# Converting every weight piece on its own: three X tiles for two, five M tiles for four

## The chip, the core and the metric

The kernel runs on one NeuronCore of a Trainium2 chip. The metric is the device time of one execution in microseconds (us), the median of the runs. The engines named below: PE (TensorE, matrix products and transposes), DVE (VectorE), ACT (ScalarE), POOL (GpSimd) and SP (SyncE, which issues nearly all DMAs here). Each works through its own queue in order; semaphores tie them together.

## What is computed

Attention with normed queries and keys, then a Fourier mixing over sequence and features, then a two-layer feed-forward part, for 8 batches of 448 tokens with 12 heads of 64 (so 768 features and 3072 hidden ones). Cut to what matters:

```python
q_n, k_n = rmsnorm(q, g_q), rmsnorm(k, g_k)
attn = softmax(q_n @ k_n.T / 8)              # per head, 448 x 448
x = attn @ v                                 # heads side by side: 8 x 448 x 768
u = x + real(fft(fft(x, axis=1), axis=2))
un = (u - mean(u)) / sqrt(var(u) + 1e-6)
out = u + relu(un @ w_ch1) @ w_ch2           # 768 x 3072 and 3072 x 768
```

The two weight matrices arrive as float64. Everything else is float32.

## The kernel before

**Work per batch.** `aux(b)` makes batch b's attention, its folding and Fourier step (`spectral`) and the normed rows `un`. `ffn(b)` is the feed-forward part: 24 products `h` (`up`, 18 matmuls each, by a w1 piece) and 36 products `o` (`down`, 12 matmuls each, by a w2 piece). `ffn_input(b, ...)` stands between them: it transposes `un` on PE into the six tiles `unT`, each rounded by ACT and completed by DVE with the remainder, since each float32 factor is split in a high and a low half and every product takes three passes. The program is: `aux(0)` with the first steps of `aux(1)` mixed in, then for each b the parts `ffn(b)` and `aux(b + 1)` merged.

**Weights.** A w1 piece is 128 hidden columns, `(m,)`; a w2 piece is 128 output columns of 512 hidden rows, `(g, d)`. In batch 0 every piece is converted from its double words and stored to HBM (`piece_kept`); later batches load what was stored. The conversion is `bits_of` and then `convert`:

- SP loads the double words into a `wide` tile (tag X; `dbl` in the profile, `dble` for pieces that are converted early, during `aux(0)`), L780;
- ACT makes the absolute high word (L783, into a tile of tag M, `mag` or `mage`) and scales the low word in place (L784);
- DVE clamps (L785), shifts (L789) and merges the sign (L793), and POOL adds the low word (L797); then the X tile is free for the next load;
- ACT rounds the value into the piece's tile (L802), DVE subtracts for the low half (L803), SP stores both halves (L839).

Before, w1 pieces are converted singly (768 values, 1536 words of 4 bytes), but w2 pieces in twos: `w2_doubles(g, d)` loads two neighbouring pieces at once (1024 values, 2048 words), and `value_of` hands the second half to the neighbour from the dictionary `mates`. There are 2 X tiles of 2048 words and 4 M tiles of 1024. From batch 2 on, tags X and M hold the tiles of `fold` as well.

**Order.** The code is written in program order, but a planner that follows a simulated timeline sets the order of each engine's queue, within the dependencies and the tiles that are free. So other tile counts and sizes can move any instruction.

Names: `mag_0_4` is the M tile of piece `(4,)` read for batch 0, `mag_0_0_4` that of piece `(0, 4)`; `mage4_3` is that of the early piece `(4, 3)`. `u0_1`, `un0_1`, `xr0_1` and `x0_100` belong to the four groups of rows of batch 0, `unT0_5` is the sixth transposed tile, `h0_0` and `o0_5_1` are products.

Of the kernel before, what the change touches and what calls it, by code (L numbers as in the profile page):

```python
# [13 lines left out]
U32 = mybir.dt.uint32  # L14
# [77 lines left out]
def spectral_block(ctx, tc, q, k, v, g_q, g_k, w1, w2, d1, d2, out, nb=B):  # L92
# [4 lines left out]
    sb = ctx.enter_context(tc.tile_pool(name="sb", bufs=2))  # L97
# [32 lines left out]
    def behind(ins):  # L130

        others = given.get(ins.ins.engine, [])
        if starting[0] and len(others) > LAG:
            order(
                ins, others[-1 - LAG],
                mybir.DependencyClass.NoSync, mybir.DependencyReason.DATA,
            )
# [15 lines left out]
            turn[0] += 1  # L153
        return ps.tile([128, 512], F32, tag=tag, name=name, bufs=BANKS[tag])

    SLOTS = {"P": 8, "PT": 6, "M": 4, "unT": 6, "h": 6}

    def slot(tag, name, dtype=F32):
        n = 1024 if tag == "M" else 900
        t = sb.tile([128, n], dtype, tag=tag, name=name, bufs=SLOTS[tag])  # L160
        return t if dtype == U32 else t[:, :900]

    def wide(name, dtype=F32):
        return sb.tile([128, 2048], dtype, tag="X", name=name, bufs=2)

    def sub(o, a, b_):
        V.tensor_tensor(out=o, in0=a, in1=b_, op=ALU.subtract)
# [38 lines left out]
    def load_dft():  # L206
        nc.sync.dma_start(D1.rearrange("r i a n -> r (i a n)"), d1)
        st = slot("PT", "d2s")[:N1, : 4 * N1].rearrange("s (n t) -> s n t", n=4)
        for r in rows_of(N1):
            nc.sync.dma_start(st[r], d2[r].rearrange("s (n t) -> s n t", n=4))  # L210
        d2v = D2.rearrange("s i c a t -> s (i c) a t")
        A.copy(d2v[:, :, 0], st)
        sub(d2v[:, :, 1], st, d2v[:, :, 0])
# [166 lines left out]
    def softmax_pair(b, p, Pc):  # L380
        QT, KD, _ = ready[b, p]
        late = b < EARLY
        if late:
            sums[b, p] = sb.tile([C, NC, 2], F32, tag="sums", name=f"sums{b}_{p}")
        for c in range(NC):
            P = slot("P", f"P{b}_{p}_{c}")[:C, : 2 * S]
            Ph = [P[:, :S], P[:, S:]]
            mn = sb.tile([C, 2], F32, tag="mn", name=f"mn{b}_{p}_{c}", bufs=4)
# [51 lines left out]
    def divide_pair(b, p, xT):  # L440

        rs = sums.pop((b, p))
        flat = rs.rearrange("t c h -> t (c h)")
        V.tensor_scalar(out=flat, in0=flat, scalar1=1e-9, scalar2=None, op0=ALU.add)
        V.reciprocal(flat, flat)
        wide_ = slot("PT", f"rs{b}_{p}")[:C, : NC * 128].rearrange(
            "t (c h d) -> t c h d", c=NC, h=2
        )
        G.tensor_copy(wide_, rs[:, :, :, None].broadcast_to([C, NC, 2, D]))
        rt = bank("PT", f"rt{b}_{p}")  # L450
        for c in range(NC):
            nc.tensor.transpose(
                rt[:, c * C : (c + 1) * C],
                wide_[:, c].rearrange("t h d -> t (h d)"), ident[:C, :C],
            )
        V.tensor_tensor(
            out=xT[:, p, :S], in0=rt[:, :S], in1=xT[:, p, :S], op=ALU.mult
        )
# [121 lines left out]
    def fold(b, p, xT, EO):  # L580
# [5 lines left out]
        if kept is not None:  # L586
            eo = slot(kept, f"eo{b}_{p}")
        else:
            if p % 2 == 0:
                halves[b] = wide(f"eo{b}_{p}")  # L590
            eo = halves[b][:, p % 2 * 900 : p % 2 * 900 + 900]
# [174 lines left out]
    w1w, w2w = w1.bitcast(U32), w2.bitcast(U32)  # L766
    kept1 = [dram.tile([128, 2, NR, 128], F32, name=f"w1_{m}") for m in range(NF)]
    kept2 = [dram.tile([128, NR, 2, 4, 128], F32, name=f"w2_{g}") for g in range(NG)]
    def bits_of(src, name):

        _, c, f = src.shape
        bits = slot("M", f"mag{name}", U32)[:, : c * f // 2].rearrange(
            "r (c f) -> r c f", c=c
        )
        raw = wide(f"dbl{name}", U32)[:, : c * f].rearrange(
            "r (c f w) -> r c f w", c=c, w=2
        )
        nc.sync.dma_start(raw.rearrange("r c f w -> r c (f w)"), src)  # L780
        low, high = raw[:, :, :, 0], raw[:, :, :, 1]
        value = bits.bitcast(F32)
        behind(nc.scalar.activation(value, high.bitcast(F32), AF.Abs))  # L783
        behind(nc.scalar.activation(low, low, AF.Copy, scale=2.0**-29))  # L784
        behind(nc.vector.tensor_scalar(  # L785
            out=value, in0=value, scalar1=MIN_HIGH, scalar2=MAX_HIGH,
            op0=ALU.max, op1=ALU.min,
        ))
        behind(nc.vector.tensor_scalar(  # L789
            out=bits, in0=bits, scalar1=5, scalar2=2,  # L790
            op0=ALU.logical_shift_left, op1=ALU.logical_shift_right,
        ))
        behind(nc.vector.scalar_tensor_tensor(  # L793
            out=bits, in0=high, scalar=0xC0000000, in1=bits,
            op0=ALU.bitwise_and, op1=ALU.bitwise_or,
        ))
        behind(nc.gpsimd.tensor_tensor(out=bits, in0=bits, in1=low, op=ALU.add))  # L797
        return value
# [6 lines left out]
        ))  # L805

    early = set()
    mates = {}

    def value_of(p, name):  # L810

        if len(p) == 1:
            return bits_of(w1_doubles(*p), name)
        if p not in mates:
            g, d = p[0], p[1] & ~1
            both = bits_of(w2_doubles(g, d), name)
            for i in range(2):
                mates[g, d + i] = both[:, :, i * 128 : i * 128 + 128]
        return mates.pop(p)

    class Stream:

# [13 lines left out]
        def converted(self, p, name):  # L836
            hl = self.tile(p, name)
            convert(value_of(p, name), [hl[:, k] for k in range(2)])
            nc.sync.dma_start(piece_kept(p), hl.bitcast(F32))  # L839
            return hl  # L840
# [13 lines left out]
    def w1_doubles(m):  # L854
        return w1w[:, m * 256 : (m + 1) * 256].rearrange("(c r) f -> r c f", r=128)

    def w2_doubles(g, d):
        return w2w[g * 512 : (g + 1) * 512, d * 256 : (d + 2) * 256].rearrange(
            "(f r) e -> r f e", r=128
        )  # L860

# [297 lines left out]
```

## Time and profile before

| | |
|---|---|
| median of 3 runs | 2140.9 us (2140.07 to 2142.75) |
| the profiled execution | 2144.78 us, span 2143.0 us |
| PE busy | 2074.9 us (97%) |
| DVE busy | 1548.4 us (72%) |
| ACT busy | 1023.3 us (48%) |
| POOL busy | 342.1 us (16%) |
| mean granted TensorE clock | 0.984 |

Busy time is the union of an engine's instructions. Batch 0's conversions lie between 20 and 440 us of the span; `ffn(0)` begins at 177 us and `ffn(1)` at 431 us. Rows of a waits view say which engine and tile waited for what, with the sum, the count and the longest wait.

### The profile page before, as it was taken

Reading aid. Unit: us, or ns where it says so; the run is one execution under the profiler, and the core shown is the slowest. Engines: PE = TensorE matmul, PEld = TensorE weight load, DVE = VectorE, ACT = ScalarE, POOL = GpSimd, SP = SyncE. Lnnn points to the kernel's source line nnn. Section 1 sums busy time; section 2 is a strip of 40 time slices with the busy share of each in tenths; the row PEclk is TensorE's granted clock in tenths of the full one; section 3 lists DMA queues with packets and bytes.
Section 4 is the critical chain, followed back from the end, with each engine's and each line's share of the span. In section 5 each row is a group of like instructions: output and inputs, shape, how many; then the busy total and the mean of one; then the engine's idle time right before and its main releaser. Section 6 shows DMA issues by size and latency. Waiting matters only on the chain.

```text
span 2143.0 us, 31181 instructions
## 1 busy us (share of the span) xinstructions
PE 2074.9 (97%) x11256; PEld 1846.7 (86%) x11256; DVE 1548.4 (72%) x2948; ACT 1023.3 (48%) x2182; POOL 342.1 (16%) x182
## 2 busy tenths in 40 slices
PE   7877999999999999999999999999999999999998
PEld 4546888889999999999999999999999989999998
DVE  6788888977885878757886778858787578764122
ACT  6857876446542555335542455425553455422100
POOL 3324433311110101001110111101010011000000
PEclk9987999999999999999999999999999999999999
DMA  6538876776566855658555765667556674458874
GB/s 185 184 97 297 275 263 220 269 237 189 174 180 189 235 165 174 187 183 231 156 175 176 240 181 169 179 194 229 166 177 189 190 206 138 152 174 253 233 251 150
DMA packets 283550, 423.86 MB, mean 198 GB/s; under 512 B 181075, under 2 KB 200516, under 8 KB 283396
## 3 DMA queue, kind: packets, MB, share of 16 engines
q1 hardware_dynamic: 278962, 419.75, 63.8%
q10 hardware_dynamic: 4434, 2.11, 0.4%
q8 instruction: 90, 1.47, 0.3%
q14 instruction: 64, 0.52, 0.1%
HBM read 362.01 MB, written 65.31 MB: 199 GB/s over the span
## 4 chain that ended last, share of the span: by engine, by line
PE 81%; DVE 6%; DMA 5%; ACT 3%; issue 2%; POOL 1%; SPq 1%; DVEq 0%; POOLq 0%; ACTq 0%
PE h L1039 29%; PE o L1060 29%; PE S L409 5%; PE av L521 4%; PE pt L509 4%; DMA dbl<-w 2%; PE y L646 2%; PE qk L345 1%; DMA w<-w 1%; PE av L483 1%; DMA ur<-u_dram 1%; ACT P L115 1%; PE oT L996 1%; PE x L677 1%; PE un L908 1%
## 5 line engine op out<-in xcount | busy, mean ns | idle before, releaser
L1039 PE MATMUL h<-unT,w 128*128 128x448 f32 x3456 | 792.0, 372 | 3.4 <-DVE unT L115 1.4
L1060 PE MATMUL o<-hs,w 128*128 128x448 f32 x3456 | 786.4, 371 | 3.1 <-DVE acc L115 1.5
L1039 PEld LDWEIGHTS h<-unT,w 128*128 128x128 f32 x3456 | 638.9, 189 | 57.8 <-DVE unT L115 1.7
L1060 PEld LDWEIGHTS o<-hs,w 128*128 128x128 f32 x3456 | 635.9, 188 | 58.6 <-issue 3.4
L115 ACT ACTIVATE P<-S,mn 112x448 f32<-112x448 f32 x384 | 244.1, 638 | 232.6 <-DVE mn L115 226.7
L115 DVE TENSOR_REDUCE mn<-S 112x1 f32<-112x448 f32 x384 | 232.8, 616 | 47.9 <-PE S L409 38.3
L115 ACT ACTIVATE hs<-h 128x448 fp32r<-128x448 f32 x192 | 104.2, 543 | 299.0 <-PE h L1039 298.2
L115 DVE TENSOR_TENSOR acc<-o,acc 128x448 f32<-128x448 f32 (+1 forms) x240 | 146.9, 614 | 126.6 <-PE o L1060 125.0
L115 DVE SCALAR_TENSOR_TENSOR hs<-h,hs 128x448 fp32r<-128x448 f32 x192 | 119.0, 620 | 139.7 <-ACT hs L115 138.6
L115 POOL TENSOR_TENSOR qkn<-raw 112x1024 f32<-112x1024 f32 x36 | 68.6, 1904 | 679.3 <-PE qk L345 606.1
L115 POOL TENSOR_TENSOR ss<-ss,nhalf 112x16 f32<-112x16 f32 x48 | 142.6, 2972 | 190.2 <-DVE ss L115 167.2
L115 ACT CAST T<-pt 128x448 fp32r<-128x448 f32 x216 | 113.2, 532 | 107.3 <-PE pt L509 105.0
L521 PE MATMUL av<-T,vhl 128*128 128x448 f32 x432 | 151.0, 382 | 0.0
L115 DVE TENSOR_TENSOR T<-pt,T 128x448 fp32r<-128x448 f32 x216 | 131.4, 616 | 25.8 <-ACT T L115 24.7
L115 DVE TENSOR_SCALAR P<-P,sm 112x448 f32<-112x448 f32 x288 | 126.6, 479 | 3.8
L409 PE MATMUL S<-KD,QT 128*112 128x448 f32 x328 | 126.5, 386 | 0.6 <-ACT P L115 0.5
L509 PE MATMUL pt<-ident,P 112*128 112x112 f32 x864 | 124.8, 259 | 0.0
L409 PE MATMUL S<-rounded,QT 128*112 128x448 f32 x328 | 119.9, 366 | 0.0
L509 PEld LDWEIGHTS pt<-ident,P 112*128 112x128 f32 x864 | 103.5, 140 | 16.3 <-DVE R L115 0.3
L115 POOL TENSOR_TENSOR rstd<-st,nhalf 112x1 f32<-112x1 f32 (+2 forms) x32 | 20.2, 632 | 507.7 <-DVE st L115 507.7
L797 POOL TENSOR_TENSOR mag<-mag,dbl 128x768 uint32<-128x768 uint32 (+1 forms) x33 | 75.9, 2301 | 140.6 <-DVE mag L793 93.5
L521 PEld LDWEIGHTS av<-T,vhl 128*128 128x128 f32 x432 | 80.9, 188 | 8.3
(120 smaller groups left out, 2501.4 us busy)
## 6 DMA issues: line engine op xcount, KB each, us to landing
w<-w SPq DMA_DIRECT2D x192, 768.0 KB, 4.9
w<-w SPq DMA_DIRECT2D x288, 512.0 KB, 4.4
dbl<-w SPq DMA_DIRECT2D x20, 768.0 KB, 4.7
dbl<-w SPq DMA_DIRECT2D x13, 1024.0 KB
raw<-q SPq DMA_DIRECT2D x96, 112.0 KB, 3.8
raw<-k SPq DMA_DIRECT2D x96, 112.0 KB, 4.6
values<-v SPq DMA_DIRECT2D x96, 96.0 KB, 4.2
u_dram<-u SPq DMA_DIRECT2D x24, 336.0 KB, 3.8
```

The source lines that it names most:

```text
L115: ins = emit(*args, **kwargs)
L345: nc.tensor.transpose(pt[:, c * C : (c + 1) * C], qk[:, i, c].rearrange("t h d -> t (h d)"), ident[:C, :C],)
L409: ins = nc.tensor.matmul(s_, QT[:, h, cs], K[:, h], start=step == 0, stop=step == 1)
L483: nc.tensor.matmul(av[:, :S], vhl[:, 3 * h + j].rearrange("s h d -> s (h d)"), T, start=h + j == 0, stop=False,)
L509: nc.tensor.transpose(pt[:, c * C : (c + 1) * C], Pc[c][:, 512 * h + j * 128 : 512 * h + (j + 1) * 128], ident[:C, :C],)
L521: nc.tensor.matmul(av[:, :S], lv, T[:, i], start=(j == 0 and i == 0), stop=False)
L646: nc.tensor.matmul(o, src[:, par, t0 : t0 + n], D1[:, ri, par, cols], start=i != 1, stop=i != 0,)
L677: nc.tensor.transpose(xp[:n, i * 128 : (i + 1) * 128], src[:, 3 * half + i], ident)
L797: behind(nc.gpsimd.tensor_tensor(out=bits, in0=bits, in1=low, op=ALU.add))
L908: nc.tensor.transpose(pt[:, OFFS[i] : OFFS[i] + LENS[i]], uns[i][:, p * 128 : (p + 1) * 128], ident[: LENS[i], : LENS[i]],)
L1039: pace(nc.tensor.matmul(o, w[:, a, c], unT[c][:, z], start=n == 0, stop=n == 17))
L1060: pace(nc.tensor.matmul(o, w[:, a, f], hs[4 * g + f][:, z], start=n == 0, stop=n == 11))
```

## The change

Pairs are gone: `w2_doubles` loads one piece (1024 words, 512 KB), `value_of` converts it alone, and `mates` goes. X has three tiles of 1800 words, M has five of 900.

```diff
-    SLOTS = {"P": 8, "PT": 6, "M": 4, "unT": 6, "h": 6}
+    SLOTS = {"P": 8, "PT": 6, "M": 5, "unT": 6, "h": 6}
 
     def slot(tag, name, dtype=F32):
-        n = 1024 if tag == "M" else 900
-        t = sb.tile([128, n], dtype, tag=tag, name=name, bufs=SLOTS[tag])
-        return t if dtype == U32 else t[:, :900]
+        return sb.tile([128, 900], dtype, tag=tag, name=name, bufs=SLOTS[tag])
 
     def wide(name, dtype=F32):
-        return sb.tile([128, 2048], dtype, tag="X", name=name, bufs=2)
+        return sb.tile([128, 1800], dtype, tag="X", name=name, bufs=3)
...
-    mates = {}
 
     def value_of(p, name):
 
         if len(p) == 1:
             return bits_of(w1_doubles(*p), name)
-        if p not in mates:
-            g, d = p[0], p[1] & ~1
-            both = bits_of(w2_doubles(g, d), name)
-            for i in range(2):
-                mates[g, d + i] = both[:, :, i * 128 : i * 128 + 128]
-        return mates.pop(p)
+        return bits_of(w2_doubles(*p), name)
...
     def w2_doubles(g, d):
-        return w2w[g * 512 : (g + 1) * 512, d * 256 : (d + 2) * 256].rearrange(
+        return w2w[g * 512 : (g + 1) * 512, d * 256 : (d + 1) * 256].rearrange(
```

What the planner makes of it, at three places. The line numbers of the changed kernel are smaller by 2 to 8, and the last number of a name only counts tiles.

**ACT's queue at the end of `aux(0)`**, from the first group's last step to the first rounded `unT`. Before:

```order
L115 ACTIVATE xr0_0_1430,st0_2_1466<-un0_2_1480 111x768
L802 CAST w1_0_0_1545<-mag_0_0_1546 128x768
L783 ACTIVATE mag_0_1_1559<-dbl_0_1_1560 128x768
L784 ACTIVATE dbl_0_1_1560<-dbl_0_1_1560 128x768
L115 ACTIVATE un0_1_1511<-u0_1_1495,st0_1_1496 112x768
L783 ACTIVATE mag_0_2_1572<-dbl_0_2_1573 128x768
L784 ACTIVATE dbl_0_2_1573<-dbl_0_2_1573 128x768
L115 ACTIVATE xr0_1_1497,st0_1_1496<-un0_1_1511 112x768
L115 ACTIVATE un0_3_1527<-u0_3_1513,st0_3_1514 112x768
L115 ACTIVATE xr0_1_1497,st0_3_1514<-un0_3_1527 112x768
L802 CAST w2_0_1_1558<-mag_0_1_1559 128x768
L115 CAST unT0_0_1617<-un0_0_1612 128x448
```

The same stretch of ACT's queue now, from the conversion of piece `(2,)`:

```order
L781 ACTIVATE mag_0_2_1617<-dbl_0_2_1618 128x768
L782 ACTIVATE dbl_0_2_1618<-dbl_0_2_1618 128x768
L115 ACTIVATE un0_1_1556<-u0_1_1540,st0_1_1541 112x768
L800 CAST w2_0_1_1603<-mag_0_1_1604 128x768
L781 ACTIVATE mag_0_4_1632<-dbl_0_4_1633 128x768
L782 ACTIVATE dbl_0_4_1633<-dbl_0_4_1633 128x768
L115 ACTIVATE xr0_1_1542,st0_1_1541<-un0_1_1556 112x768
L115 ACTIVATE un0_3_1572<-u0_3_1558,st0_3_1559 112x768
L781 ACTIVATE mag_0_0_0_1645<-dbl_0_0_0_1646 128x512
L782 ACTIVATE dbl_0_0_0_1646<-dbl_0_0_0_1646 128x512
L115 ACTIVATE xr0_1_1542,st0_3_1559<-un0_3_1572 112x768
L115 CAST unT0_0_1662<-un0_0_1657 128x448
```

Four instructions of the conversion, those of pieces `(4,)` and `(0, 0)`, now stand ahead of the first `unT`; before they came after the fifth. Piece `(2,)` now stands ahead of `un0_1`.

**SP's queue in the same stretch**, from the rows of group 2 to the load of piece `(0, 0)`. Before:

```order
L690 DMA u_dram_77<-u0_2_1465 15x768
L780 DMA dbl_0_1_1560<-w1 128x6x256
L780 DMA dbl_0_2_1573<-w1 128x6x256
L839 DMA w2_4_114<-w2e4_2_1448 128x1024
L839 DMA w2_4_114<-w1e4_3_1461 128x1024
L690 DMA u_dram_77<-u0_1_1495 112x768
L839 DMA w1_0_86<-w1_0_0_1545 128x1536
L690 DMA u_dram_77<-u0_3_1513 112x768
L780 DMA dbl_0_4_1588<-w1 128x6x256
L851 DMA w2_0_3_1584<-w1_3_89 128x1536
L780 DMA dbl_0_0_0_1601<-w2 128x4x512
```

SP's queue now (the load of piece `(1,)` stands two rows ahead of the first of these):

```order
L688 DMA u_dram_77<-u0_2_1510 15x768
L831 DMA w2_4_114<-w2e4_2_1484 128x1024
L778 DMA dbl_0_2_1618<-w1 128x6x256
L778 DMA dbl_0_4_1633<-w1 128x6x256
L688 DMA u_dram_77<-u0_1_1540 112x768
L831 DMA w2_4_114<-w1e4_3_1497 128x1024
L778 DMA dbl_0_0_0_1646<-w2 128x4x256
L843 DMA w2_0_3_1629<-w1_3_89 128x1536
```

The loads of pieces `(4,)` and `(0, 0)` moved ahead of the stores of `u0_3` and of the converted piece `(0,)`.

**PE's queue where `ffn(0)` ends**, around the transposes of batch 1's last group of rows. Before:

```order
L1060 MATMUL o0_5_1_4123<-hs0_23_4100,w2_0_5_1_3889 128x448 x3
L677 MATMUL x1_100_3982<-ident_68,xr1_1_3980 112x128 x3
L677 MATMUL x1_101_3987<-ident_68,xr1_1_3980 112x128 x3
L1060 MATMUL o0_5_2_4139<-hs0_20_3707,w1_0_5_2_3952 128x448 x3
...
L1060 MATMUL o0_5_3_4155<-hs0_23_4100,w2_0_5_3_4022 128x448
L677 MATMUL x1_110_4028<-ident_68,xT1_1698 112x128 x3
L677 MATMUL x1_111_4033<-ident_68,xT1_1698 112x128 x3
L1060 MATMUL o0_5_3_4155<-hs0_23_4100,w2_0_5_3_4022 128x448 x2
```

PE's queue now; the transposes of `x1_100` stand further up, inside `o0_5_0`:

```order
L1052 MATMUL o0_5_1_4285<-hs0_23_4253,w2_0_5_1_4024 128x448 x3
L675 MATMUL x1_110_4181<-ident_68,xT1_1752 112x128 x3
L675 MATMUL x1_111_4186<-ident_68,xT1_1752 112x128 x3
L1052 MATMUL o0_5_2_4301<-hs0_20_3833,w1_0_5_2_4096 128x448 x3
```

The last transposes of `x1` stand 22 feed-forward matmuls earlier, so more products are left to run behind them.

## Rows read from the trace of the kernel before

**Rows 1.** Stretches of the span: each engine's busy us, PE clock, DMA share, GB/s.

```profile
0.00:150.00 150.00, 118.86 (x572) 75.15 (x573) 113.58 (x191) 99.65 (x223) 53.05 (x34) 0.87 0.55 163
150.00:185.00 35.00, 16.85 (x76) 13.69 (x75) 31.69 (x58) 24.11 (x41) 12.77 (x8) 0.66 0.62 217
185.00:350.00 165.00, 162.51 (x833) 136.34 (x832) 139.85 (x205) 128.36 (x242) 66.54 (x31) 1.00 0.84 280
350.00:440.00 90.00, 83.80 (x435) 72.96 (x434) 85.86 (x121) 47.66 (x78) 32.41 (x15) 0.98 0.63 221
440.00:2000.00 1560.00, 1556.06 (x8663) 1422.27 (x8663) 1143.28 (x2314) 714.21 (x1584) 177.33 (x94) 1.00 0.63 190
2000.00:2143.00 143.00, 136.77 (x685) 126.24 (x683) 34.11 (x62) 9.28 (x17) 0.00 (x0) 0.99 0.67 206
```

**Rows 2.** Waits of PE, 350 to 440 us: sum us, times, longest.

```profile
PE un L908 <- ACT un L115: 2.3, 1, 2.3
PE y L646 <- DVE eo L115: 1.5, 1, 1.5
PE o L1060 <- DVE acc L115: 1.5, 1, 1.5
PE h L1039 <- DVE hs L115: 0.7, 1, 0.7
```

**Rows 3.** Waits of PE, 150 to 185 us.

```profile
PE un L908 <- ACT un L115: 8.5, 3, 3.4
PE x L677 <- ACT xr L115: 6.4, 1, 6.4
```

**Rows 4.** Waits of ACT, 150 to 440 us.

```profile
ACT mag L783 <- DMA dbl<-w: 30.1, 18, 4.7
```

**Rows 5.** DMA issues: tile, queue, count, KB each, us to landing.

```profile
dbl<-w SPq DMA_DIRECT2D x20, 768.0 KB, 4.7
dbl<-w SPq DMA_DIRECT2D x13, 1024.0 KB
...
dble<-w SPq DMA_DIRECT2D x5, 1024.0 KB
```

**Rows 6.** Timeline of DVE: start, us, line, shapes; conversions of 768 and 1024 values.

```profile
182.98 0.56 DVE L785 TENSOR_SCALAR mag<-mag 128x768 f32<-128x768 f32 x1 [0.23 <-ACT mag L783]
...
184.76 0.95 DVE L793 SCALAR_TENSOR_TENSOR mag<-dbl,mag 128x768 uint32<-128x768 uint32 x1
187.72 0.69 DVE L785 TENSOR_SCALAR mag<-mag 128x1024 f32<-128x1024 f32 x1 [2.01 <-ACT mag L783]
...
189.17 1.23 DVE L793 SCALAR_TENSOR_TENSOR mag<-dbl,mag 128x1024 uint32<-128x1024 uint32 x1
```

**Rows 7.** Groups of ACT by shape: count, busy us, mean ns, idle before.

```profile
L783 ACT ACTIVATE mag<-dbl 128x768 f32<-128x768 f32 x20 | 18.2, 912 | 21.0 <-DMA dbl<-w 17.8 <-DVE acc L115 3.2
...
L783 ACT ACTIVATE mag<-dbl 128x1024 f32<-128x1024 f32 x13 | 14.9, 1149 | 16.9 <-DMA dbl<-w 12.3 <-DVE w L803 4.5
```

**Rows 8.** Timeline of POOL: the adds of the early pair and of piece (1,).

```profile
158.75 2.37 POOL L797 TENSOR_TENSOR mage<-mage,dble 128x1024 uint32<-128x1024 uint32 x1 [22.34 <-DVE mage L793]
...
172.35 1.85 POOL L797 TENSOR_TENSOR mag<-mag,dbl 128x768 uint32<-128x768 uint32 x1 [2.73 <-issue]
```

**Rows 9.** Timeline of ACT: piece (2,), the first four casts of unT, the sixth.

```profile
171.45 0.91 ACT L783 ACTIVATE mag<-dbl 128x768 f32<-128x768 f32 x1 [0.62 <-DMA dbl<-w]
...
176.39 1.82 ACT L115 CAST unT<-un 128x448 fp32r<-128x448 f32 x4
...
183.66 0.52 ACT L115 CAST unT<-un 128x448 fp32r<-128x448 f32 x1
```

**Rows 10.** Chain of work that ended last: start, us, what; loads of double words.

```profile
178.43 8.02 DMA dbl<-w
...
393.14 5.97 DMA dbl<-w
...
410.52 6.37 DMA dbl<-w
```

## The prediction

> **What bounds the kernel now.** I read the busy time by stretches first [rows 1]. It shows one kernel with four parts. From 440 us on PE is busy 1556.1 of 1560 us at full clock, so nothing that the conversions do can be felt there. From 185 to 350 us it is busy 162.5 of 165 us, also at full clock: `ffn(0)` and `aux(1)` fill it, while DVE has 165 - 139.9 = 25.1 us free and ACT 36.6 us. Only two parts are not held by PE. The first is 0 to 185 us, where PE is busy 118.9 of 150 and then 16.9 of 35 us, the granted clock is 0.87 and 0.66, and DVE is the fullest engine beside PE (113.6 of 150 us, then 31.7 of 35 us). The second is 350 to 440 us, where DVE is busy 85.9 of 90 us and PE 83.8.
>
> Then I read whom PE waits for in these two parts. From 350 to 440 us there are four single waits, for the folded tiles, an accumulator, `un` and `hs` of the last product: 1.5 + 1.5 + 2.3 + 0.7 = 6.0 us [rows 2]. All come from DVE or from ACT behind DVE. From 150 to 185 us PE waits for `un` and `xr`, 8.5 + 6.4 us [rows 3]: the last steps of `aux(0)`, one group of rows after the other, before the feed-forward part can begin. PE never waits long for a weight piece there. But ACT does: 18 times and 30.1 us in all it stands before a conversion whose double words have not landed [rows 4], and what is queued behind that conversion stands too.
>
> **What the singles cost.** There are 13 + 5 = 18 pairs [rows 5], so 36 single conversions take their place. DVE's price of a conversion follows the length with a fixed part: L785 takes 0.56 us for 768 values and 0.69 for 1024, L793 0.95 and 1.23 [rows 6]. A line through the two gives 0.43 and 0.67 us for 512; L789 is priced like L785. Two singles against a pair: 2 x (2 x 0.43 - 0.69) + (2 x 0.67 - 1.23) = 0.34 + 0.11 = 0.45 us, 18 pairs 8.1 us. Rounding and subtracting were done by pieces before and stay. On ACT 912 and 1149 ns [rows 7] give 675 ns for 512, so 2 x (2 x 675 - 1149) = 0.40 us per pair and 7.2 us in all. On POOL 1.85 and 2.37 us [rows 8] give 1.33, so 0.29 us per pair, 5.2 us in all, on an engine that is 16% busy. SP issues 18 DMAs more; it waits for tiles most of the time, and no load is on PE's path in the parts that PE fills.
>
> DVE has 54 instructions more, and the rows put the fixed part at 0.15 us each. [...]
>
> **Part one, 0 to 150 us.** Four of the five early pairs fall here: 4 x 0.45 = 1.8 us on DVE. The stage is a mesh of short dependencies in which DVE is busy 76% [rows 1], so I charge that share: +1.4 us. It could be all 1.8 us; and since a POOL add is now 1.0 us shorter for what waits behind it (2.37 to 1.33 us), the lower end is -1.0.
>
> **Part two, 150 to 185 us.** Here the planner's order decides. With a third X tile it loads pieces `(4,)` and `(0, 0)` earlier and puts their ACT and DVE steps ahead of the first `unT`. On ACT that is 2 x 0.91 + 2 x 0.675 = 3.2 us, on DVE 0.56 + 0.56 + 0.95 + 0.43 + 0.43 + 0.67 = 3.6 us. The work is not extra, it stood behind `unT` before. But the ACT steps of `(0, 0)` also wait for its load, and `unT` now waits behind them, and PE for `unT`. That load needs the X tile of piece `(1,)`, free after POOL's add, which ended at 172.35 + 1.85 = 174.2 us [rows 8]. I put that 1.5 us earlier, at 172.7, since the early pair is now halved ahead of it (1.0 us on POOL, 0.5 on L793). Loads of double words are on the chain with 8.02, 5.97 and 6.37 us [rows 10]; this one has two thirds of the bytes of a w1 piece, so I take 4.0 to 8.0 us. It lands at 176.7 to 180.7. Two ACT steps (1.35 us) and `xr` (0.85) follow: the first `unT` at 178.9 to 182.9 against 176.4 [rows 9], 2.5 to 6.5 us late. The sixth `unT`, which the first product needs as well, was held back before until 183.7 us by piece `(4,)` [rows 9]. Now it follows the first by five casts of 0.45 us and three of pieces, 2.3 us: 183.5 to 187.5, that is -0.2 to +3.8 us. I take +2.0, the middle of what the sixth says, as PE can't finish the product before it; the ends for the range are -0.2 and +6.5 (the first `unT`'s). The casts of pieces that stood behind it are then done, but PE hardly waited for those.
>
> **Part three, 185 to 350 us.** About eight of the pairs, 3.6 us more DVE work, lie beside a full PE with 25.1 us of DVE time free: 0. If PE lost its fill (a late piece), the cover would go; the loads are earlier, not later, so I keep 0.
>
> **Part four, 350 to 440 us.** DVE has 4.1 us free, and the chain of work that ended last runs here through the X tiles: POOL's add, a load of 5.97 us, ACT, DVE, POOL, a load of 6.37 us [rows 10]. A third tile lets the next load start before that add. Ahead of the last steps of `aux(1)` the order now has as much conversion on DVE as before, counted from the first folded tile on, but PE's transposes of `x1` stand 22 matmuls earlier, with more products behind them to cover what follows. Against that stand five of the 18 pairs, 2.3 us more on a DVE that is nearly full. I take -1.5 us: a quarter of the 6.0 us of waits, because DVE's total ends the stage and not the loads alone. The ends are -6.0 (all waits gone) and +2.3 (the added work in full).
>
> **Part five, after 440 us.** No conversions. From batch 2 on `fold` uses tags X and M, and the planner puts some transposes of queries up to 94 places earlier or later, in even and odd batches in turn as before. PE has them behind products all the time: 0.
>
> The sum: 1.4 + 2.0 + 0 - 1.5 + 0 = +1.9 us, on the profiled execution 2144.8 + 1.9 = 2146.7 us. That one lies 3.9 us above the median of the runs, 2140.9, so the forecast is 2142.8 us. A measurement of this kernel can tell about 0.2%, 4.3 us, from no change: 2136.6 to 2145.2 is "the same".
>
> **The rivals.**
>
> The load chain was the limit of part four, and of part two. Then the third tile takes out the 6.0 us of waits, part two comes out at -0.2, and part one at its lower end, -1.0, would add to it; with part one at +1.4 it is -4.8, so 2136.1 us. For it: ACT's 30.1 us of waiting for double words [rows 4] and the two loads on the chain. Against it: DVE is busy 85.9 of 90 us there whatever the loads do. [...]
>
> The load of `(0, 0)` decides part two: it lands late, ACT's queue stands, and the whole `unT` series comes 6.5 us late, with nothing of part four in return: 1.4 + 6.5 = +7.9 us, 2148.8 us, slower. It decides as soon as the load needs over 6 us from a tile that is free at 172.7. For it: the order now puts the loads of `(2,)`, `(4,)` and `(0, 0)` close together, and a load in this stretch already took 8.02 us [rows 10]. Against it: it is the smallest of these loads.
>
> DVE's added work counts in full in parts one to four, with no cover: +8.1 us, 2149.0 us. Against it: 25.1 us of free DVE time in part three.
>
> The change does not do what it says: SP's queue is in order, so a load for the third tile can stand behind a store that waits, and start no sooner. Then only the fixed parts are left in parts one and four, 1.4 + 2.3 = +3.7 us, 2144.6, still the same within the measurement; it is part of the forecast's chance.
>
> **How the numbers follow.** Forecast (all that ends within 0.2%) 0.47, load chain 0.25, late load 0.20, full DVE work 0.08. Faster 0.25, same 0.47, slower 0.28. The ends of all terms give -7.2 and +10.6 us; not all come together, so the range reaches to the rivals' times, 2135.5 to 2149.
>
> **What would show it.** Right: PE's waits for `un` and `xr` from 150 to 185 us longer by about 2 us with the first `unT` at 179 us or later; PE as full as before from 185 to 350 us; the PE waits from 350 to 440 us somewhat under 6.0 us; L785 at 0.43 us and L793 at 0.67 for 512 values. Wrong: the first product starting earlier than 177 us, since then the third tile has shortened the end of `aux(0)`; PE waits from 350 to 440 us near zero or over 8 us; or a difference that only appears after 440 us, where I have nothing.

## The result

The changed kernel takes 2162.96 us (median of 4 runs, 2161.29 to 2164.82); the kernel before, beside it, 2141.82 us (2140.07 to 2145.45). The ratio is 1.0097, with a 95% interval of 1.0079 to 1.0114: 21 us slower, outside the range of the prediction.

The stretches of the changed kernel, with the columns of [rows 1]:

```profile
0.00:150.00 150.00, 115.81 (x525) 70.53 (x526) 110.76 (x197) 99.18 (x227) 58.74 (x38) 0.86 0.55 163
150.00:185.00 35.00, 17.38 (x97) 14.70 (x95) 28.36 (x59) 22.18 (x38) 11.28 (x7) 0.74 0.48 155
185.00:350.00 165.00, 156.00 (x784) 130.93 (x785) 143.31 (x221) 126.38 (x248) 67.53 (x40) 0.96 0.81 265
350.00:440.00 90.00, 79.10 (x394) 67.65 (x392) 80.47 (x117) 44.49 (x84) 31.49 (x17) 0.92 0.68 218
440.00:2000.00 1560.00, 1557.96 (x8695) 1428.24 (x8694) 1166.52 (x2349) 726.03 (x1602) 184.19 (x99) 1.00 0.62 190
2000.00:2159.50 159.50, 153.54 (x768) 141.82 (x766) 35.30 (x63) 12.50 (x23) 0.00 (x0) 0.99 0.67 212
```

PE is no longer full from 185 to 350 us (156.0 of 165 us against 162.5) and emptier from 350 to 440 us (79.1 against 83.8), with the granted clock at 0.96 and 0.92 where it was 1.00 and 0.98. After 440 us it is as full as before. DVE isn't fuller in the fourth stretch but emptier: 80.5 against 85.9 us. (The stretches are fixed in time; the same work comes 7 to 22 us later in the changed kernel.)

The lag of the changed kernel at the same piece of PE work, from both timelines, dates the loss. The last two columns are runs that come below, in their profiled execution; that of the halves in the order of before is the fastest of its ten (2135.74 us, median 2139.50), so a few us of its lead are chance:

| PE work | before, us | changed | halves, own order | halves, order of before |
|---|---|---|---|---|
| last `y` | 149.5 | +7.2 | +6.9 | -1.3 |
| first `h0_0` | 177.0 | +9.9 | +5.3 | -2.9 |
| 519th feed-forward matmul | 350.1 | +14.1 | +8.8 | -5.6 |
| 806th | 440.0 | +22.4 | +12.0 | -5.8 |
| 6254th | 2000.1 | +16.9 | +7.4 | -9.1 |

So 7 us are lost by 150 us, 3 up to the first product, 4 up to 350 us, and 8 up to 440 us. The lag that shrinks again after 440 us is mostly not the kernel's doing: executions of one program lie up to 7 us apart (2139.2 to 2146.2 us for the kernel before, over all runs), and the profiled one of before lies high in that. The halves in the order of before have the same order there and shrink by 3.3 us too.

The prices were right only in part. Groups by shape, 0 to 450 us of the changed kernel: count, busy us, mean ns, idle before.

```profile
L791 DVE SCALAR_TENSOR_TENSOR mag<-dbl,mag 128x512 uint32<-128x512 uint32 x26 | 19.7, 763 | 0.2
...
L783 DVE TENSOR_SCALAR mag<-mag 128x512 f32<-128x512 f32 x26 | 13.8, 532 | 4.2 <-ACT mag L781 4.1
...
L791 DVE SCALAR_TENSOR_TENSOR mage<-dble,mage 128x512 uint32<-128x512 uint32 x10 | 6.8, 685 | 0.0
...
L783 DVE TENSOR_SCALAR mage<-mage 128x512 f32<-128x512 f32 x10 | 4.2, 420 | 0.0
...
L781 ACT ACTIVATE mag<-dbl 128x512 f32<-128x512 f32 x26 | 17.5, 671 | 3.8 <-DMA dbl<-w 2.8 <-DVE w L801 1.0
...
L795 POOL TENSOR_TENSOR mag<-mag,dbl 128x512 uint32<-128x512 uint32 x25 | 37.1, 1486 | 82.7 <-DVE mag L791 19.0 <-DVE ss L115 13.1 <-ACT w L800 11.3
L795 POOL TENSOR_TENSOR mage<-mage,dble 128x512 uint32<-128x512 uint32 x10 | 21.8, 2191 | 39.3 <-DVE mage L791 27.4 <-ACT T L115 4.8 <-ACT KD L115 2.8
```

DVE's 0.69 and 0.42 us for the early singles and ACT's 0.67 us were forecast as 0.67, 0.43 and 0.675. But the 26 later singles take 0.76 and 0.53 us on DVE, and POOL's adds 2.19 us (early) and 1.49 us (later) against 1.33. In all, the three DVE steps of the w2 pieces (L783, L787, L791) take 63.1 us against 52.2 before: 10.9 us more, where 8.1 were forecast.

### Two places of the loss

**At 110 us.** The timeline of the changed kernel, POOL's, then DVE's and ACT's: start, us, what, in brackets the idle time before and its releaser.

```profile
110.82 6.84 POOL L795 TENSOR_TENSOR mage<-mage,dble 128x512 uint32<-128x512 uint32 x2 [6.71 <-DVE mage L791]
```

```profile
113.58 1.26 DVE L115 TENSOR_SCALAR sums<-sums 112x8 f32<-112x8 f32 x1
```

```profile
114.85 0.62 ACT L800 CAST w2e<-mage 128x512 fp32r<-128x512 f32 x1 [2.08 <-POOL mage L795]
115.38 0.52 ACT L115 COPY T<-pt 128x448 f32<-128x448 f32 x1
117.69 0.62 ACT L800 CAST w1e<-mage 128x512 fp32r<-128x512 f32 x1 [1.79 <-POOL mage L795]
118.22 0.97 ACT L115 COPY T<-pt 128x448 f32<-128x448 f32 x2
```

ACT's queue has the casts of the two early pieces between the copies `T` of the attention. Each cast waits for its own POOL add, and the two adds take 6.84 us together; PE stands at its products `av` for the `T` behind them. Before, one add of 3.17 us stood there, and both casts followed it with one wait:

```profile
108.03 3.17 POOL L797 TENSOR_TENSOR mage<-mage,dble 128x1024 uint32<-128x1024 uint32 x1 [6.75 <-DVE sums L115]
```

```profile
111.23 0.62 ACT L802 CAST w2e<-mage 128x512 fp32r<-128x512 f32 x1 [2.37 <-POOL mage L797]
111.75 0.61 ACT L802 CAST w1e<-mage 128x512 fp32r<-128x512 f32 x1
```

PE's waits for `T` up to 150 us grow from 7.7 to 9.4 us, and the granted clock from 90 to 125 us falls from 0.89 to 0.79. This place has only the smaller part of the first 7 us: the product `av` that starts at 110.54 us is already 4.9 us late, the last `av` behind the place 7.4. The larger part arises between 85 and 107 us, where PE now waits for `xT` (1.4 us) and `rs` (1.1 us) and before waited for neither.

**At 383 us.** PE's one long wait of the fourth stretch behind the transposes `pt` whose copies are `T`, then ACT's and DVE's timeline ahead of it:

```profile
380.54 0.93 PE L474 MATMUL pt<-ident,P 112*128 112x112 f32 x8
387.70 1.86 PE L481 MATMUL av<-T,values 128*128 128x448 f32 x2 [6.23 <-ACT T L115]
```

```profile
382.92 0.19 ACT L115 COPY xT<-xT 128x1 f32<-128x1 f32 x1 [3.69 <-DVE xT L115]
383.02 0.83 ACT L800 CAST w<-mag 128x768 fp32r<-128x768 f32 x1
383.75 0.52 ACT L115 COPY R<-rem 128x448 f32<-128x448 f32 x1
384.18 0.66 ACT L781 ACTIVATE mag<-dbl 128x512 f32<-128x512 f32 x1
385.01 0.63 ACT L115 ACTIVATE KD<-qk,gains 64x448 fp32r<-64x448 f32 x1 [0.17 <-DVE rounded L115]
385.67 0.56 ACT L115 CAST KD<-KD 64x448 fp32r<-64x448 f32 x1
386.26 0.83 ACT L800 CAST w<-mag 128x768 fp32r<-128x768 f32 x1
387.12 0.97 ACT L115 COPY T<-pt 128x448 f32<-128x448 f32 x2
```

```profile
379.12 0.95 DVE L801 TENSOR_TENSOR w<-mag,w 128x768 fp32r<-128x768 f32 x1
379.99 0.20 DVE L115 RECIPROCAL sums<-sums 112x8 f32<-112x8 f32 x1
380.10 1.11 DVE L115 TENSOR_TENSOR eo<-sd 128x452 f32<-128x452 f32 x2
381.13 0.69 DVE L791 SCALAR_TENSOR_TENSOR mag<-dbl,mag 128x512 uint32<-128x512 uint32 x1
381.74 0.62 DVE L115 TENSOR_TENSOR acc<-o,acc 128x448 f32<-128x448 f32 x1
382.27 0.62 DVE L115 TENSOR_TENSOR xT<-rt,xT 128x448 f32<-128x448 f32 x1
```

The `T` that PE needs takes half a microsecond, and its `pt` was done at 381.5 us. Seven instructions stand ahead of it on ACT, the first of which waits 3.69 us for an `xT` that on DVE stands behind conversions and folds. ACT is busy 14.2 of the 25 us from 370 to 395 us, and DVE 24.1, no more than before (24.7); what PE needs is not at the head of their queues. Nor did it pass what stood ahead of it: ACT stood idle until 382.92 us with `pt` done at 381.5, and `T` started at 387.12, behind all seven. Both places show the order, but not yet what made it: the added work, the tiles, or any change at all.

### The profile page after: what moved, and what is told of

Read it like the earlier page. It is cut to its first block, busy times and chain, and to the rows that moved or that the text cites. A ratio compares the mean times of both kernels' runs of the same rounds, so it can differ in the third digit from the quotient of the medians.

```text
span 2159.5 us, 31363 instructions
## 1 busy us (share of the span) xinstructions
PE 2079.8 (96%) x11256; PEld 1853.9 (86%) x11256; DVE 1564.7 (72%) x3002; ACT 1030.8 (48%) x2218; POOL 353.2 (16%) x200
## 4 chain that ended last, share of the span: by engine, by line
PE 84%; DVE 6%; DMA 4%; ACT 2%; issue 2%; POOL 1%; SPq 1%; DVEq 0%; ACTq 0%; POOLq 0%
PE o L1052 30%; PE h L1031 29%; PE S L407 6%; PE av L519 4%; PE pt L507 4%; PE y L644 2%; DMA dbl<-w 2%; PE qk L343 1%; PE av L481 1%; DMA ur<-u_dram 1%; PE x L675 1%; PE un L900 1%; PE oT L988 1%; DVE mn L115 1%; PE ab L723 1%
## 5 line engine op out<-in xcount | busy, mean ns | idle before, releaser
L795 POOL TENSOR_TENSOR mag<-mag,dbl 128x512 uint32<-128x512 uint32 (+1 forms) x46 | 77.1, 1678 | 150.1 <-DVE mag L791 68.1
L481 PE MATMUL av<-T,values 128*128 128x448 f32 x144 | 75.2, 609 | 16.1 <-ACT T L115 16.1
```

Source lines behind the costliest of these rows:

```text
L481: nc.tensor.matmul(av[:, :S], vhl[:, 3 * h + j].rearrange("s h d -> s (h d)"), T, start=h + j == 0, stop=False,)
```

## The experiments

Three theories. **Work**: the added instructions and loads cost the 21 us. **Tiles**: the third X and fifth M tile let conversions into the queues too early. **Order**: the planner makes a new order for the whole program at any change, and what a new order loses is its own. All times are medians; the kernel before lay at 2142.3 to 2143.4 us beside these runs.

### Added instructions and tile counts apart

`halves` keeps loads and tiles of pairs and does the six steps in two halves:

```diff
+        whole = bits, raw
+        for part in range(2 if c == 4 else 1):
+            if c == 4:
+                cut = slice(part * 128, part * 128 + 128)
+                bits, raw = whole[0][:, :, cut], whole[1][:, :, cut]
```

The others are the changed kernel with X and M counts of 2 and 4, 3 and 4, 2 and 5:

```diff
-    SLOTS = {"P": 8, "PT": 6, "M": 5, "unT": 6, "h": 6}
+    SLOTS = {"P": 8, "PT": 6, "M": 4, "unT": 6, "h": 6}
...
-        return sb.tile([128, 1800], dtype, tag="X", name=name, bufs=3)
+        return sb.tile([128, 1800], dtype, tag="X", name=name, bufs=2)
```

> The kernel before, with pairs loaded and held as before (two X tiles of 2048, four M tiles of 1024), but each of the six conversion steps of a pair done in two halves: the added instructions of the change without its loads and tiles. Theory 'work' (the added instructions themselves cost the 21 us): 2155 to 2163 us. Theory 'tiles' (the third X tile and the fifth M tile let conversions stand earlier in the queues, and those wait): at most +4 us, 2141 to 2146. Theory 'plan' (each new order costs or gives something of its own, whatever its cause): anywhere from 2138 to 2163, with waits in other places than in the changed kernel.

> Single conversions, but the tile counts of before: two X tiles, four M tiles. Work: like the changed kernel, 2158 to 2165 us. Tiles: 2141 to 2147, as the loads can't run further ahead than before (each load is smaller, so rather less is under way). Plan: anywhere from 2138 to 2170, with no order by tile count among this run and the next two.

> Single conversions, three X tiles, four M tiles: the third X tile alone. Work: 2158 to 2165 us. Tiles: it is the X tile that starts loads earlier, so about the changed kernel's time, 2157 to 2165, and at least 10 us over the run with two and four. Plan: anywhere from 2138 to 2170.

> Single conversions, two X tiles, five M tiles: the fifth M tile alone. Work: 2158 to 2165 us. Tiles: M tiles are held from the absolute value to the subtraction, longer than X tiles, but a load needs both, so with two X tiles little changes: 2141 to 2150. Plan: anywhere from 2138 to 2170.

| run | us | ratio | 95% interval |
|---|---|---|---|
| halves | 2154.03 | 1.0047 | 1.0032 to 1.0062 |
| singles, 2 X and 4 M | 2155.72 | 1.0055 | 1.0038 to 1.0072 |
| singles, 3 X and 4 M | 2156.47 | 1.0058 | 1.0043 to 1.0073 |
| singles, 2 X and 5 M | 2150.43 | 1.0029 | 1.0018 to 1.0041 |

Neither "work" nor "tiles" gives these: about half of the loss is there without any new tile, the third X tile alone adds nothing, and the fifth M tile alone takes some away, yet both together cost the most. All four lag by 7 to 10 us at 150 us, so I took one swap at 95 us for their common cause.

### One swap, one part, and no change of work at all

`rs-first` puts POOL's power of `ss1_0` back behind the copy `rs0_3`. `early-pairs` leaves the five early pairs alone (with two X and four M tiles). The two nulls change one number of the kernel before and add nothing.

```diff
+        if (b, p) == (1, 0):
+            order(
+                power, spread[3],
...
-CONVERT_EARLY = 0.12
+CONVERT_EARLY = 0.125
...
-RATIO_FIRST = 0.6
+RATIO_FIRST = 0.59
```

> The changed kernel with one order put in by hand: on POOL the power of ss1_0 (2.9 us) stands behind the copy rs0_3, as in the kernel before; in the changed kernel it stands ahead of it, and PE's in-order queue stands at the transposes of rs0_3 with the last scores behind them. Theory 'order at 95 us' (that swap makes the 7 us by which the changed kernel is late at 123 us): the lag of the last product of attention at 123 us falls from 7.3 to 3 us or less, and the time is 2154 to 2159 us, if nothing later is replanned for the worse. Theory 'work' (the added instructions make it): lag still about 7 us, 2160 to 2166 us.

> Tiles of before (two X, four M); the five early pairs stay pairs, every later w2 piece is converted singly. Order at 95 us: rs0_3 stands ahead of ss1_0 on POOL as before, so the lag at 123 us is 1 us or less, and what is left is what later singles cost: of the 12 us that singles with two and four tiles cost, 7 to 8 go, 2144 to 2150 us. Work: 26 of 36 singles are left, 0.7 of 12 us, spread over the stages: 2150 to 2153 us with some lag at 123 us already.

> The kernel before with one number changed: the share of a piece that is converted per step of the first batch is 0.125 in place of 0.12. No instruction is added; but on POOL ss1_0 now stands ahead of rs0_3, as in the changed kernel. Order at 95 us: a lag of 4 to 8 us at 123 us without any single, 2145 to 2153 us. Work: no lag, 2139 to 2146 us.

> The kernel before with one number changed: the side work of the next batch is mixed into the first feed-forward part at a ratio of 0.59 in place of 0.6. No instruction is added, and the order up to 200 us is that of before. It shows how far a new order alone moves the time after 200 us. Work: 2139 to 2146 us. Plan (each new order costs or gives something): lag 0 to 200 us, and then up to 10 us in either direction, 2135 to 2152.

| run | us | ratio | 95% interval |
|---|---|---|---|
| rs-first | 2162.04 | 1.0093 | 1.0078 to 1.0109 |
| early-pairs | 2157.05 | 1.0069 | 1.0054 to 1.0084 |
| null-early | 2161.71 | 1.0090 | 1.0075 to 1.0105 |
| null-ratio | 2150.00 | 1.0035 | 1.0020 to 1.0049 |

My swap was at most a small part of the cause: with `rs-first` the last scores come 2.9 us late and not 5.8, but the last `av` still 6.2 us and not 7.4. `early-pairs` keeps the start (lag 0.9 us at 150 us) and loses 12.0 us in the rest, where the singles with the same tiles lose 2.1 (9.6 at 150 us, 11.7 at the end). Then the nulls, which have no instruction more: they cost 7.7 and 19.4 us. PE's waits of `null-early`, 0 to 440 us:

```profile
PE av L483 <- ACT T L115: 20.6, 12, 2.9
PE ab L725 <- ACT bs L115: 7.3, 1, 7.3
PE un L908 <- ACT un L115: 5.7, 3, 2.8
```

They are of the kind that the changed kernel has, `av` for `T` above all, but at other places: `null-early` is 7 us late already at the scores that the kernel before runs at 43 us, where the changed kernel is on time. A new order can cost that much without the change.

### The added work in the order of before

If "order" is right, the added work must be nearly free where the order is kept. So the order of the kernel before was written down, engine by engine, and put in as a chain (which moves line numbers by up to 24):

```diff
+            for x, y in zip(chain, chain[1:]):
+                tc.add_manual_dep(
+                    y, x.name,
+                    mybir.DependencyInfo(
+                        mybir.DependencyClass.NoSync, mybir.DependencyReason.DATA
+                    ),
+                    reason="issue order",
+                )
```

In `halves-old-order` the second half of each step stands right behind the first. `singles-old-order` and `pairs-new-order` chain everything but the loads and conversion steps, which the planner places freely: singles (two X, four M tiles) in the order of before, and pairs in the order of the changed kernel. `late-order` asks a side question, the gain after 440 us.

> The halves of the first group again (pairs loaded at once, each of the six steps of a pair done in two halves), but with the order of before written down for every queue; the second half of a step stands right behind the first. So only the added instructions are left of the change. Theory 'order' (new orders of the queues make the loss): what the added instructions cost in place, 1 to 5 us, 2143 to 2147 us. Theory 'work': as the halves in their own order, 2152 to 2156 us.

> Single conversions with two X and four M tiles, and the order of before written down for everything but the loads and the six steps of the conversions, which are placed freely between. Singles with these tiles in their own order took 2155.7 us. Order: 2143 to 2149 us. Work (added instructions and loads): 2153 to 2157 us.

> The reverse: the kernel before with its pairs and tiles, and the order of the changed kernel written down for everything but the loads and the six steps of the conversions. No instruction is added. Order: most of the 21 us comes with it, 2155 to 2164 us. Work: 2140 to 2147 us.

> The kernel before, its order written down up to the second feed-forward part, and behind that, from about 450 us on, the order that the planner gave to singles with two X and four M tiles. That kernel needed 1577.5 - 4.7 us where the kernel before needs 1577.5 (from the 1200th feed-forward matmul to the last). Order: 4 to 5 us faster than before, 2136 to 2139 us, with no lag before 500 us. If that gain came from the smaller tiles and not from the order: 2141 to 2144 us.

| run | us | ratio | 95% interval |
|---|---|---|---|
| halves-old-order | 2139.50 | 0.9983 | 0.9974 to 0.9993 |
| singles-old-order | 2170.46 | 1.0130 | 1.0115 to 1.0146 |
| pairs-new-order | 2181.75 | 1.0184 | 1.0167 to 1.0201 |
| late-order | 2143.40 | 1.0007 | 0.9997 to 1.0016 |

`halves-old-order` decides: the same 108 added instructions (six for each of 18 pairs) as in the halves, 14.5 us less (13.4 when each run is taken against the kernel before beside it), and 2.8 us faster than before. PE's third and fourth stretch there are as full as before again:

```profile
185.00:350.00 165.00, 164.97 (x853) 139.94 (x850) 143.61 (x236) 132.31 (x265) 72.12 (x39) 1.00 0.83 276
350.00:440.00 90.00, 83.78 (x438) 73.50 (x437) 83.95 (x137) 46.23 (x80) 35.56 (x19) 0.98 0.68 238
```

And the two POOL adds of 110 us, here at 106 us, take 3.79 us together, not 6.84:

```profile
105.95 3.79 POOL L821 TENSOR_TENSOR mage<-mage,dble 128x512 uint32<-128x512 uint32 x2 [6.23 <-DVE mage L817]
```

The two mixed orders were misses for both theories, at 28 and 39 us. I read them as telling nothing on the work: conversions that are placed freely in a queue written for others can make it wait. In `pairs-new-order` ACT's casts wait for POOL (0 to 450 us):

```profile
ACT w L817 <- POOL mag L812: 16.6, 5, 5.8
...
ACT w2e L817 <- POOL mage L812: 12.9, 6, 3.5
```

against 9.3 us for `w` before and 1.4 in the changed kernel: the casts stand where a single's add would be done, and the pair's isn't. In `singles-old-order` the waits for `w` are 4.7 us, fewer than before, and where its 28 us come from stays open. `late-order` gained nothing after 450 us: the 4.7 us had been read from single executions.

### Loads, and the spread of orders

`two-loads-old-order` also splits the pair's load in two, so that all instructions and DMAs of the change are there. The rest are three more orders: the kernel before at a ratio of 0.61, the changed kernel at 0.61, and the changed kernel with 0.122 converted per step.

```diff
+        loads = 2 if c == 4 else 1
+        for part in range(loads):
+            cut = slice(part * f // loads, (part + 1) * f // loads)
...
-RATIO_FIRST = 0.6
+RATIO_FIRST = 0.61
...
-CONVERT_EARLY = 0.12
+CONVERT_EARLY = 0.122
```

> The halves in the order of before once more, and the pair's load is split as well: two loads of 512 KB into the two halves of the X tile, one behind the other on SP. So all instructions and DMAs of the change are there, in the order of before. Theory 'order': the halves took 2139.5 us; the first half of a conversion can now start when its own 512 KB are there, so 0 to 3 us faster than that, 2136 to 2140 us. Theory 'loads' (18 more DMAs in SP's queue make part of the loss): 2143 to 2152 us.

> The kernel before with the mixing ratio of the first feed-forward part at 0.61 in place of 0.6; no instruction added. The other two orders of this kernel cost 7.7 and 19.4 us. Theory 'before is an exceptional order': slower than before again, by 4 to 15 us and all of it after 180 us, 2146 to 2157. Theory 'orders scatter about before': faster or slower, 2134 to 2150 with either sign.

> The changed kernel with the mixing ratio at 0.61 in place of 0.6: the same singles, three X and five M tiles, another order after 180 us. If the tile counts make the loss beyond that of singles with two and four tiles: 2159 to 2167 us, like the changed kernel. If it is the order alone: anywhere in the spread of the singles' orders so far, 2150 to 2167 us, and the lag at 180 us unchanged at 10 us.

> The changed kernel with the share converted per step of the first batch at 0.122 in place of 0.12: the same singles and tiles, another order from the start. If the tile counts make the loss: 2159 to 2167 us. If it is the order alone: anywhere from 2148 to 2170 us, with another lag at 180 us than the 10 us of the changed kernel.

| run | us | ratio | 95% interval |
|---|---|---|---|
| two-loads-old-order | 2140.53 | 0.9994 | 0.9986 to 1.0003 |
| null-ratio-up | 2148.43 | 1.0029 | 1.0019 to 1.0040 |
| after-ratio-up | 2159.52 | 1.0081 | 1.0066 to 1.0097 |
| after-early-up | 2156.25 | 1.0065 | 1.0051 to 1.0078 |

With its loads too, the work of the change makes no difference in the order of before. Twelve orders were planned anew, three of them without added work, and all are slower: 1.0029 to 1.0097 in all, 1.0029 to 1.0090 for the three. The changed kernel's own three orders lie at 1.0065 to 1.0097. So before's order is an exceptional one, and the changed kernel lies at the far end of a spread that one nudged number nearly reaches as well (1.0090).

### Which stretch

The halves once more, with the order of before written down for the part up to 185 us alone (`old-start`), and for the part behind that alone (`old-rest`). The two kernels differ only in the table of the written order: on PE it holds the first 636 of 10972 instructions in `old-start` and the other 10336 in `old-rest`.

> The halves with the order of before written down up to about 185 us (the start of the first feed-forward part) and planned freely from there. The halves took 2154.0 us in their own order and 2139.5 in that of before, 14.5 us apart; at 177 us of the kernel before their lags were +5.3 and -2.9 us, 8.2 apart. If order decides in each stretch by itself: the start is won, lag about -3 at 180 us, and the rest costs the other 6 us or what another new order costs there (4 to 12): 2143 to 2152 us. If only the order at the start matters: 2138 to 2142 us.

> The reverse: the halves planned freely up to about 185 us, and the order of before written down for all that follows. If order decides in each stretch by itself: the lag at 180 us is that of the halves, 5 to 8 us, it neither grows nor shrinks much afterwards, and the time is 8 us above the 2139.5 us, 2145 to 2150 us. If a later stretch takes in what the start lost: 2138 to 2143 us.

`old-start` took 2153.31 us (1.0048, 1.0032 to 1.0063), `old-rest` 2153.64 us (1.0048, 1.0031 to 1.0065), 1.3 and 3.6 us over what was expected. Their lags show where. `old-rest` is 9.2 us late at the first product (the free start came out worse than that of the halves, 5.3), and then 9.7, 9.8 and 8.0 us at the last three marks of the table: with the order of before nothing is lost behind the start, and nothing given back. `old-start` is 0.6 us early at the first product and then 1.6 late at 350 and 5.1 at 440 us; its profiled execution is the fastest of its four (2149.91 us), so these lags are some us too small. Each stretch loses by its own order. That the losses add up isn't shown: by the medians `old-start` loses 10.6 us, `old-rest` 10.9, and the halves in their own order 10.6 as well, and the part that was planned anew came out otherwise each time.

## Why the prediction was wrong, point by point

- **The forecast** (2142.8 us) and all rivals priced the change's own work and waits. None had the price of a new order as such, though the diff of the queues showed instructions moved nearly everywhere. That is the step that failed: I costed the moves at three places and took the rest for unchanged. In its place the runs showed 5.8, 7.7 and 19.4 us for three new orders without any added work.
- **The added work**, 8.1 us on DVE, of which 3 to 4 us were to be felt: the three steps take 10.9 us more in the changed kernel and 4.2 us more in `halves-old-order`, and in the order of before nothing of it is felt (0.9983, and 0.9994 with the loads split). "DVE's full work" (2149.0) is refuted with it. The gain of 2.8 us with 108 instructions more has the sign of part one's lower end; whether shorter steps let waiting work in sooner, as I argued there, was not tested.
- **Part one**, +1.4 us with ends of -1.0 and +1.8: it lost 7.2. The error is in the ends: they were worked out from the added DVE time and a shorter POOL add. But 4.9 us were lost between 85 and 107 us, and 2.5 us at 110 us, where ACT's queue stands for POOL, both in an order that I hadn't compared there; and the POOL adds at 110 us are not shorter, 6.84 us for two against 3.17 for one.
- **Part two**, +2.0 us: 2.7 us, as the first product's lag grows from 7.2 to 9.9. The first `unT` starts at 186.34 us against 176.39 [rows 9], the sixth at 192.73 against 183.66; less the 7.2, 2.7 and 1.9 us late. The size holds, with some luck: it came by another load than the one that was priced (and the middle of -0.2 and +3.8 is 1.8, not 2.0). DVE had `st` ready for `un0_1` at 176.88 us, but piece `(2,)`, which now stands ahead of it on ACT, waited for its load, so `un0_1` starts 1.8 us later:

```profile
176.68 0.20 DVE L115 TENSOR_SCALAR st<-st 112x1 f32<-112x1 f32 x1
```

```profile
177.07 0.89 ACT L781 ACTIVATE mag<-dbl 128x768 f32<-128x768 f32 x1 [2.24 <-DMA dbl<-w]
...
178.66 0.92 ACT L115 ACTIVATE un<-u,st 112x768 f32<-112x768 f32 x1
```

PE's waits, 150 to 200 us, are 11.3 and 5.4 us where [rows 3] have 8.5 and 6.4:

```profile
PE un L900 <- ACT un L115: 11.3, 3, 6.3
PE x L675 <- ACT xr L115: 5.4, 1, 5.4
PE h L1031 <- ACT unT L115: 2.1, 1, 2.1
PE h L1031 <- DVE unT L115: 2.1, 1, 2.1
```

- The late load of `(0, 0)` did not decide it: ACT waited 0.61 us for it. The load chain was no gain either: ACT's waits for `mag` fall from 30.1 [rows 4] to 14.8 us (0 to 450 us), but those for the second step, `dbl`, rise from 10.3 to 22.9, and PE gained nothing.
- **Part three**, 0: the lag grew from 9.9 to 14.1 us. "PE is full, so nothing is felt" named the cover and what would remove it (a late piece); what removed part of it was a conversion in the way. PE's longest wait from 185 to 350 us ends at DVE's `rounded` (239.97 to 240.66 us), and ahead of that ACT waits for double words and DVE for ACT's `mag`:

```profile
PE o L1052 <- DVE rounded L115: 2.5, 1, 2.5
```

```profile
237.17 0.90 ACT L782 ACTIVATE dbl<-dbl 128x768 uint32<-128x768 uint32 x1 [1.49 <-DMA dbl<-w]
```

```profile
238.65 0.43 DVE L783 TENSOR_SCALAR mag<-mag 128x512 f32<-128x512 f32 x1 [2.40 <-ACT mag L781]
```

- **Part four**, -1.5 us with ends of -6.0 and +2.3: 8.3 us lost. PE's waits are 10.9 us where [rows 2] have 6.0, over the 8 us that I had named as "wrong":

```profile
PE av L481 <- ACT T L115: 6.8, 2, 6.2
PE y L644 <- DVE eo L115: 2.4, 1, 2.4
PE o L1052 <- DVE hs L115: 1.7, 1, 1.7
```

The transposes of `x1` do stand earlier, with more products behind them, as said; but the `T` of 383 us is a place that I hadn't looked at.
- **Part five**, 0: right within what executions of one kernel differ.

What stays open: whether three X and five M tiles have a share of their own. All four orders with these counts (the changed kernel's three and `rs-first`, 1.0065 to 1.0097) lie above the three of singles with fewer tiles (1.0029 to 1.0058), so a share of up to half of the loss isn't excluded; on the other side `early-pairs` (1.0069) and `null-early` (1.0090) lie among them with the tiles of before. The changed kernel in the order of before wasn't run: in that order the two X tiles can hold four w2 pieces at once, and three tiles of one piece hold three. Nor is it known why the planner's new orders are all worse than that of the kernel before.

## What to carry to other kernels

Where a planner orders the queues, a change of sizes or tile counts is a new order of everything: time a null first (a number nudged, no work changed), since its spread, 0.3 to 0.9% here, is the least uncertainty of any forecast for it. Work and order come apart by writing the old order down and adding the work in place; only then does a price per instruction say what a change costs. And a loss ahead of a stretch that PE fills stayed nearly whole to the end: 9.2 us at the first product of `old-rest`, 8.0 at 2000 us.

## What was not expected of the hardware

A POOL add of 512 values takes 1.28 us at one place (381.95 us of the changed kernel), where DVE runs `acc<-o,acc` and `xT<-rt,xT` beside it (above). Two take 6.84 us at 110 us, where DVE runs `sd<-eo` and `mage<-dble,mage` back to back. A DVE instruction on 112x8 values took 1.26 us there, until 114.84 us, when ACT's cast behind the first of the two adds begins (114.85); the same takes 0.17 us in a quiet place (107.71 us of the kernel before). What made the adds and that instruction long isn't shown: no run here tested it by itself.
